# Second up-projection: seven products for eight in two of three token groups, and a plain group at the end

## The chip, the cores and the metric

One NeuronCore of a Trainium2 chip runs the whole program. The metric is device time in microseconds (us), the median of several runs. The engines are TensorE (PE, with its weight loads as PEld), VectorE (DVE), ScalarE (ACT), GpSimd (POOL, which only builds masks here) and SyncE (SP, whose queue issues all DMAs).

## What is computed

Chunked attention with eight memory keys, then two feed-forward layers on 3072 tokens of width 512, with an inner width of 2048, all in float32:

```python
out[:, :, c_start:c_end] = np.matmul(a, v_full)      # attention, per chunk of 32
...
h = x @ w_in;  r = np.maximum(h, 0.0);  g = s * (r * r) + b;  x = g @ w_out
...
h = x @ w_in2;  g = h - np.tanh(h);  return g @ w_out2
```

The change concerns `h = x @ w_in2` and `g = h - tanh(h)`, called **up 2** below. Before it stand attention, up 1 and **down 1** (`g @ w_out`), after it **down 2** (`g @ w_out2`).

## The kernel before

**Products.** A float32 operand is split in two float32r halves, a high one (ACT copies with rounding) and a low one (DVE subtracts the high one from the source). `three` (L149 to L152) multiplies with three matmuls of 128x512: high times high, low weight times high, high weight times low. A step on "one product" below means calls of `three`.

**Down 1 and down 2** (class `Down`, L447) use a two-by-two scheme of seven products P1 to P7 over halves of the inner and output dimensions. A pass p goes through one product for the three token groups g (1024 tokens each) in 12 entries of 12 matmuls. `run` (L608) issues for entry i: the split of entry i+2 (`split`, L554, ACT then DVE, into a ring of three buffers), a load of a later part (`load_to`, L495, SP), the matmuls (`multiply`, L571), then weight steps and `between`. The right-hand sides of down 2 were stored to `o2` by up 2 as seven combined operands and are loaded back as parts (p, g, h), where h is the half of the eight blocks n.

**Up 2** goes over eight blocks n of 256 columns of `w_in2` (L1016). In each block, groups g=0 and g=1 are computed plainly: per group two row tiles i and two columns `col`, each a `plain_column` (L934) of 4x3 = 12 matmuls, 48 in all; `plain_end` (L941) takes tanh on ACT and subtracts on DVE in tiles of 128x1024. Group g=2 is computed by `quad` (L959) as seven products of 6 matmuls, 42 in all. P1, P6, P5 and P3 accumulate in one PSUM bank, P7 and P4 in a second, P2 in a third, and snapshots of the first bank are copied out by ACT (L968) between them; DVE adds make the other outputs (L971), and each 128x512 output has its own tanh and subtract (L977, L978). The operands of P4 to P7 are sums of token quarters, T1 to T4, made on DVE at the end of down 1 (`b_t1` to `b_t3`, L666 to L674, and L698) and split by `t_split` (L861); the weight sums are made per block by `w2_sums` (L811) and split by `w2_split` (L823).

**Output of up 2.** `end_out` (L928) combines four outputs on DVE with four subtractions (`combine`, L437) and stores the pair of tiles `oa` and `ob`; two pairs are used in turn (`C_OT`). The eight PSUM banks are `bank(0)` to `bank(7)`; `bank2(2)` is banks 4 and 5, `bank2(3)` banks 6 and 7.

**What sets the order.** The program order of the kernel is the order on each engine (`manual_schedule`, L740); an instruction that waits holds all behind it on its engine. Tables place side work: `READY` (L64) prepares `w_out2` during down 1, `WEIGHTS` (L51) the weights of each pass.

```python
for n in range(8):
    ...
    for col in range(2):
        plain_column(n, 0, 0, col)
    ...
    group = quad(n)
```

Of the kernel before, what the change touches and what calls it, by code (L numbers as in the profile page):

```python
# [58 lines left out]
for q in (2, 5, 6):  # L59
# [24 lines left out]
def tile_chunk_attention_two_ffn(  # L84
# [86 lines left out]
    def filled_in_raw(z, raw):  # L171
# [21 lines left out]
    X2 = {"Q": ("E13", "E14", "E15"), "V": ("E16", "E17"),  # L193
          "X": (("Z9", "Z10"), ("Z2", "Z3"), ("Z4", "Z6")), "U": ("E6", "E7", ("Z0", "Z1"))}
    B_TMP = ("E16", "E17", "Z8")
    C_RAW, C_Z, C_W = "E0", "Z5", ("E1", "E2")
    C_OT = (("E3", "E11"), ("E9", "E12"))
    C_R = ("Y0", "Y1")
    C_T = {"T3": "E8", "T2": "E5", "T1": "E10", "T4": "E4"}
    C_SHL, C_SNAP = ("Y3", "Y4"), ("Y2", "Z7")  # L200
    Z2 = {("A11", 0): "Z8", ("A11", 1): "Y5", ("A21", 0): "Z11", ("A21", 1): "Z9",
          ("A22", 0): "Z10", ("A22", 1): "Z2", ("A12", 0): "Y3", ("A12", 1): "Y4"}
    D_WHL = (("E13", "E16"), ("E2", "E3"))
    D_STREAM = ("E6", "E17", "E14", "E7", "E11")
    D_RING = ("E8", "E5", "E10")
    D_S = (("Z4", "Z6"), ("Z0", "Z1"))
    D_ACC = {"X": ("Z7", "Z5", "Z3"), "U": ("Y0", "Y1", "Y2"), "V": ("E4", "E4", "E12")}
    D_OUT = ("E9", "E15")
# [238 lines left out]
    class Down:  # L447


        def __init__(self, src, zmap, smap, whl, stream, ring, load, view, pick, bias, final, turn):  # L450
# [4 lines left out]
            self.loaded, self.turn, self.ahead = 0, turn, 1 - 2 * turn  # L455
            self.parts = [(p, g, h) for p in range(7) for g in range(NG) for h in range(2)]
            self.entries = [(p, g, h, e) for p, g, h in self.parts for e in range(2)]
            self.quads = list(zmap)

        def load_quadrant(self, raw_place):  # L460
# [3 lines left out]
            def place_z():  # L464
                place = self.zmap[key]
                if isinstance(place, tuple):
                    if place[1] == 0:
                        self.zt[place[0]] = new(place[0], 2048, F32, "zq")
                    z = self.zt[place[0]][:, 1024 * place[1]:1024 * (place[1] + 1)]
                else:  # L470
                    z = new(place, 1024, F32, "zq")
                self.z[key] = z
                return z

            def begin():
                scaled(place_z(), raw)
# [12 lines left out]

        def load_words(self):  # L490
            key = self.quads.pop(0)
            z = self.z[key] = new(self.zmap[key], 1024, F32, "zq")
            nc.sync.dma_start(out=z, in_=wz[2 * ("A11", "A21", "A12", "A22").index(key[0]) + key[1]])

        def load_to(self, n):  # L495
            while self.loaded <= min(n, len(self.parts) - 1):
                i = self.loaded
                p, g, h = self.parts[i]
                self.part[i] = new(self.stream[i % len(self.stream)], 4 * NB, F32, "part")
                self.load(self.part[i], ORDER[p], g, h)  # L500
                self.loaded += 1
# [164 lines left out]
    def b_t3():  # L666
        b_f["T3"] = new(C_R[1], 2 * NB, F32, "t3").rearrange("p (m t) -> p m t", m=2)
        minus(b_f["T3"], b_f["Q"], b_f["V"])

    def b_t1():  # L670
        minus(b_f["V"], b_f["V"], b_f["X"])

    def b_t2():
        minus(b_f["Q"], b_f["Q"], b_f["V"])  # L674

    def final1(name, g, ps):
        a = lambda k: sums1.at(k, g)

        def last_sum(k, x, op):
# [5 lines left out]
            if g == NG - 1:  # L685
                b_f[k] = o
# [3 lines left out]
            def halves():  # L690
# [6 lines left out]
                if g == NG - 1 and k == "U":  # L697
                    minus(o, o, b_f["Q"])  # L698
# [27 lines left out]
        b_c[:, 0:1], final1, 0,  # L726
# [96 lines left out]
    def w2_split(n):  # L823
        hi, lo = (new(p_, 1024, F32R, "shl") for p_ in C_SHL)
# [23 lines left out]
    def between1(p, k):  # L848
# [37 lines left out]
    def final2(name, g, ps):  # L886
# [29 lines left out]
        None, final2, 1,  # L916
# [17 lines left out]
    def plain_column(n, g, i, col):  # L934
        ps = bank2(2 + i)
        wh, wl = wi[2, n]
        for c in range(KD):
            xh, xl = x2_of(c, 1 - col, g)
            three(ps[:, col, 0:NB], wh[:, i, c, :], wl[:, i, c, :], xh, xl, c == 0, c == KD - 1)

    def plain_end(n, g, i):  # L941
        ps = bank2(2 + i)
        oa = outs[n, g][0]
        r = new(C_R[i], 2 * NB, F32, "r2").rearrange("p (m t) -> p m t", m=2)
        nc.scalar.activation(out=r, in_=ps[:, :, 0:NB], func=AF.Tanh)
        nc.vector.tensor_tensor(out=oa[:, 2 * i:2 * i + 2], in0=ps[:, :, 0:NB], in1=r, op=ALU.subtract)
# [4 lines left out]
    def strassen(name):  # L951
        acc = bank(chain[name])
        wh, wl = w2_hl[name]
        xh, xl = x2[operand[name], NG - 1]
        new_ = name in ("P1", "P7", "P2")
        for c in range(2):
            three(acc, wh[:, c], wl[:, c], xh[:, c], xl[:, c], c == 0 and new_, c == 1, not new_)

    def quad(n):  # L959
        g = NG - 1  # L960
        begin_out(n, g)
        oa = outs[n, g][0]
        keep = new(C_SNAP[0], 2 * NB, F32, "keep")
        snap = {1: keep[:, 0:NB], 2: keep[:, NB:2 * NB], 3: new(C_SNAP[1], NB, F32, "keep3")}
        rs = {}

        def copy(q):
            nc.scalar.activation(out=snap[q], in_=bank(0), func=AF.Copy)  # L968

        def add(o, q, k):  # L970
            nc.vector.tensor_tensor(out=oa[:, o], in0=snap[q], in1=bank(k), op=ALU.add)  # L971

        def curve(o, src):
            if o // 2 not in rs:
                rs[o // 2] = new(C_R[o // 2], 2 * NB, F32, "r2").rearrange("p (m t) -> p m t", m=2)
            r = rs[o // 2][:, o % 2]
            nc.scalar.activation(out=r, in_=src, func=AF.Tanh)  # L977
            nc.vector.tensor_tensor(out=oa[:, o], in0=src, in1=r, op=ALU.subtract)  # L978

        strassen("P1")  # L980
        copy(1)
        yield
        strassen("P7")
        strassen("P6")
        copy(2)
        yield
        strassen("P5")
        copy(3)
        strassen("P2")
        add(2, 3, 1)  # L990
        strassen("P3")
        add(1, 1, 2)
        strassen("P4")
        yield
        curve(0, bank(0))
        curve(1, oa[:, 1])
        curve(2, oa[:, 2])
        add(3, 2, 1)
        curve(3, oa[:, 3])
        yield  # L1000
        end_out(n, g)
        yield

    group = None
# [11 lines left out]
    for n in range(8):  # L1016
        last = n == 7
        before = group
        begin_out(n, 0)
        for col in range(2):  # L1020
            plain_column(n, 0, 0, col)
        if before is not None:
            next(before)
        if not last:
            w2_load(n + 1)
        plain_end(n, 0, 0)
        if before is not None:
# [12 lines left out]
        begin_out(n, 1)  # L1040
# [25 lines left out]
        if last:  # L1066
            down2.split(0)
# [88 lines left out]
```

## Time and profile before

| | us |
|---|---|
| median of 3 runs | 1064.58 (1063.6 to 1066.26) |
| profiled execution | 1064.68 |
| its span, first to last instruction | 1062.7 |
| PE busy in the span | 1046.7 (98%) |
| DVE / ACT busy | 776.6 (73%) / 512.2 (48%) |
| granted clock of TensorE, mean | 0.997 |

The profiled execution is 0.10 us above the median. Busy time of PE counts matmuls that overlap, so a busy PE alone does not say that it is full; the distance from the start of one matmul to the next does. Up 2 runs from 579.6 to 829.9 us of the span, down 2 from there to the end.

### The profile page before, as it was taken

How to read it: one execution, taken by the hardware profiler on the slowest of the kernel's cores; microseconds unless marked ns; L12 is line 12 of the kernel's file. 1: busy time of each engine (PE TensorE's matmuls, PEld its weight loads, DVE VectorE, ACT ScalarE, POOL GpSimd, SP SyncE). 2: the span in 40 equal slices, each digit the busy share in tenths (PEclk: the TensorE clock that was granted, in tenths of full speed). 3: DMA queues.
4: the chain of work that ended last, by engine and by line, in shares of the span. 5: the costliest groups of instructions: out<-in, count | busy, mean ns of one | idle time of the engine just before them, and what ended most of it. 6: DMA issues, size and time to landing. Idle time of an engine off the chain costs nothing.

```text
span 1062.7 us, 15185 instructions
## 1 busy us (share of the span) xinstructions
PE 1046.7 (98%) x6048; PEld 867.8 (82%) x6048; DVE 776.6 (73%) x939; ACT 512.2 (48%) x914; POOL 2.8 (0%) x24
## 2 busy tenths in 40 slices
PE   6999999999999999999999999999999999999998
PEld 5788888888888888888888888888888888888887
DVE  7998557777657787878787767776766876776654
ACT  7886345444523564456554533333333554444432
POOL 1000000000000000000000000000000000000000
PEclk8999999999999999999999999999999999999999
DMA  9796378666458997666871266555557895556671
GB/s 320 246 336 244 137 271 293 242 246 214 178 210 316 358 338 277 206 227 221 288 261 41 98 239 247 218 208 198 213 202 272 322 374 190 192 185 248 228 267 60
DMA packets 74278, 250.54 MB, mean 236 GB/s; under 512 B 5600, under 2 KB 5856, under 8 KB 63968
## 3 DMA queue, kind: packets, MB, share of 16 engines
q1 hardware_dynamic: 74208, 249.58, 65.8%
q8 instruction: 47, 0.77, 0.3%
q14 instruction: 23, 0.19, 0.0%
HBM read 151.00 MB, written 98.57 MB: 235 GB/s over the span
## 4 chain that ended last, share of the span: by engine, by line
PE 95%; DMA 3%; DVE 1%; issue 0%; ACT 0%; SPq 0%; ACTq 0%
PE pb L150 30%; PE pb L152 30%; PE pb L151 30%; PE pb L323 2%; DMA raw<-in_wi_dram 2%; PE pb L301 2%; PE pb L261 1%; DMA part<-o 1%; DMA qk<-in_qk_dram 1%; DVE ringhringl L568 0%; ACT ringhringl L567 0%; DVE ob L439 0%; DVE oa L978 0%; DVE oa L971 0%; SPq L244 0%
## 5 line engine op out<-in xcount | busy, mean ns | idle before, releaser
L152 PE MATMUL pb<-ringhringl,whl 128*128 128x512 f32 (+1 forms) x680 | 262.9, 387 | 0.4 <-DVE ringhringl L568 0.4
L150 PE MATMUL pb<-ringhringl,whl 128*128 128x512 f32 (+1 forms) x680 | 262.9, 387 | 0.0
L151 PE MATMUL pb<-ringhringl,whl 128*128 128x512 f32 (+1 forms) x680 | 262.9, 387 | 0.0
L568 DVE TENSOR_TENSOR ringhringl<-part,ringhringl 128x1024 fp32r<-128x1024 f32 x120 | 146.7, 1224 | 81.9 <-ACT ringhringl L567 81.9
L567 ACT ACTIVATE ringhringl<-part 128x1024 fp32r<-128x1024 f32 x120 | 127.1, 1061 | 158.4 <-PE pb L152 151.3
L150 PE MATMUL pb<-xh,w 128*128 128x512 f32 (+1 forms) x392 | 153.9, 393 | 0.0
L152 PE MATMUL pb<-xl,w 128*128 128x512 f32 (+1 forms) x392 | 151.2, 386 | 0.0
L151 PE MATMUL pb<-xh,w 128*128 128x512 f32 (+1 forms) x392 | 151.0, 385 | 0.0
L152 PEld LDWEIGHTS pb<-ringhringl,whl 128*128 128x128 f32 x680 | 127.7, 188 | 26.6 <-DVE ringhringl L568 0.8
L150 PEld LDWEIGHTS pb<-ringhringl,whl 128*128 128x128 f32 x680 | 127.7, 188 | 26.0
L151 PEld LDWEIGHTS pb<-ringhringl,whl 128*128 128x128 f32 x680 | 127.7, 188 | 25.9
L414 ACT ACTIVATE r<-pb 128x512 f32<-128x512 f32 x96 | 55.4, 592 | 106.3 <-PE pb L152 93.5
L424 DVE SCALAR_TENSOR_TENSOR oa<-pb,s_c,r 128x512 f32<-128x512 f32 x96 | 70.6, 746 | 39.9 <-ACT r L414 39.7
L150 PEld LDWEIGHTS pb<-xh,w 128*128 128x128 f32 x392 | 73.6, 188 | 16.1
L285 ACT ACTIVATE sm<-sm,nmx 128x96 f32<-128x96 f32 x192 | 69.1, 362 | 36.4 <-DVE nmx L279 36.4
L152 PEld LDWEIGHTS pb<-xl,w 128*128 128x128 f32 x392 | 73.6, 188 | 15.0
L151 PEld LDWEIGHTS pb<-xh,w 128*128 128x128 f32 x392 | 73.7, 188 | 14.0
L150 PE MATMUL pb<-x2hx2l,w 128*128 128x512 f32 x192 | 74.7, 389 | 0.0
L151 PE MATMUL pb<-x2hx2l,w 128*128 128x512 f32 x192 | 74.7, 389 | 0.0
L152 PE MATMUL pb<-x2hx2l,w 128*128 128x512 f32 x192 | 74.7, 389 | 0.0
L562 ACT ACTIVATE ringhringl<-part,b_c 128x1024 fp32r<-128x1024 f32 x48 | 55.1, 1150 | 39.8 <-PE pb L152 37.3
L563 DVE SCALAR_TENSOR_TENSOR ringhringl<-part,b_c,ringhringl 128x1024 fp32r<-128x1024 f32 x48 | 61.5, 1283 | 16.9 <-ACT ringhringl L562 16.7
(134 smaller groups left out, 1351.4 us busy)
## 6 DMA issues: line engine op xcount, KB each, us to landing
o<-ob SPq DMA_DIRECT2D x48, 1024.0 KB, 4.8
part<-o SPq DMA_DIRECT2D x84, 512.0 KB, 4.9
part<-o SPq DMA_DIRECT2D x42, 1024.0 KB, 6.2
o<-oa SPq DMA_DIRECT2D x48, 768.0 KB, 3.4
raw<-in_wi_dram SPq DMA_DIRECT2D x16, 1024.0 KB, 7.8
raw<-in_wo_dram SPq DMA_DIRECT2D x16, 1024.0 KB, 7.9
qk<-in_qk_dram SPq DMA_DIRECT2D x24, 640.0 KB, 8.1
v<-in_vw_dram SPq DMA_DIRECT2D x24, 384.0 KB, 7.5
```

The costliest lines, as they stand in the source:

```text
L150: nc.tensor.matmul(acc, lhsT=whi, rhs=xhi, start=first, stop=False, skip_group_check=more)
L151: nc.tensor.matmul(acc, lhsT=wlo, rhs=xhi, start=False, stop=False, skip_group_check=more)
L152: nc.tensor.matmul(acc, lhsT=whi, rhs=xlo, start=False, stop=last, skip_group_check=more)
L285: nc.scalar.activation(out=sm[:, h, :], in_=sm[:, h, :], func=AF.Exp, bias=nmx[:, h:h + 1], scale=1.0, accum_out=sums[:, h:h + 1],)
L301: nc.tensor.transpose(out=bank(2 + g)[0:KE, P * r:P * (r + 1)], in_=sm[:, 4 * g + r, :], identity=ident)
L323: nc.tensor.matmul(value_bank(u)[64 * g:64 * g + 64, c0:c0 + QE], lhsT=tv[0:KE, e, 2 * r + g, :], rhs=pt[0:KE, 4 * g + r, QE * e:QE * (e + ...
L414: nc.scalar.activation(out=r, in_=up_ps[j, t], func=AF.Relu)
L424: nc.vector.scalar_tensor_tensor(out=oab[j, q][0][:, 2 * i:2 * i + 2, k, :], in0=ps2, scalar=s_c[:, 0:1], in1=r2, op0=ALU.mult, op1=ALU.mult,)
L562: nc.scalar.activation(out=xh, in_=src, func=AF.Identity, bias=self.bias)
L563: nc.vector.scalar_tensor_tensor(out=xl, in0=src, scalar=self.bias, in1=xh.bitcast(F32), op0=ALU.add, op1=ALU.subtract)
L567: nc.scalar.activation(out=xh, in_=src, func=AF.Copy)
L568: nc.vector.tensor_tensor(out=xl, in0=src, in1=xh.bitcast(F32), op=ALU.subtract)
```

## The change

Group g=1 of up 2 is computed by seven products as g=2 was; g=0 stays plain. The generator `quad` becomes a class `Quad` whose products, copies, adds, tanhs and subtractions are placed one by one. The two quads of a block, a and b, use banks 0, 1, 2 and banks 3, 7, 6; the second and third of b's are shared with the plain row tile 1. Snapshots 1 and 2 of both quads share one buffer (`C_SNAP`), snapshot 3 lies in `oa`; tanh is written into `ob` (or in place) instead of a buffer of its own. The next block's first plain column stands inside the quads of the block before. T1 to T4 exist for g=1 and g=2, so three more splits and four more sums are made; most are moved into passes 5 and 6 of down 1 (`SUMS`, `SPLITS`), and `READY` moves up. In the last block the plain group comes last, and down 2's first pass takes the groups in the order 1, 2, 0; its words of weights and its first parts are loaded at other places.

```diff
-    (3, 6): [("load", 5, "E7")], (4, 0): [("scale", 5, "Z9")], 
-    (4, 6): [("fill", 5), ("load", 6, "E7")], (4, 9): [("scale", 6, "Z0")], 
-    (5, 2): [("fill", 6), ("load", 7, "E7")], (5, 6): [("scale", 7, "Z1")], 
-    (5, 10): [("fill", 7)],
+    (3, 0): [("load", 5, "E7")], (3, 4): [("scale", 5, "Z9")],
+    (3, 8): [("fill", 5), ("load", 6, "E7")], (4, 2): [("scale", 6, "Z0")],
+    (4, 5): [("fill", 6), ("load", 7, "E7")], (4, 8): [("scale", 7, "Z1")],
+    (4, 11): [("fill", 7)],
 }
+SUMS = {(4, 9): [("T3", 1)], (5, 0): [("T3", 2)], (5, 9): [("T1", 1)], (5, 10): [("T2", 1)],
+        (6, 1): [("T1", 2)], (6, 2): [("T2", 2)]}
+SPLITS = {(5, 6): [("T3", 1)], (6, 5): [("T1", 1)], (6, 9): [("T4", 1)], (6, 10): [("T3", 2)], (6, 11): [("T1", 2)]}
...
-            self.parts = [(p, g, h) for p in range(7) for g in range(NG) for h in range(2)]
+            self.parts = [(p, g, h) for p in range(7) for g in (range(NG) if p else first) for h in range(2)]
...
+    banks = ((0, 1, 2), (3, 7, 6))
...
+        def place(self, q):
+            return self.oa[:, 2] if q == 3 else snap[0][:, NB * (q - 1):NB * q]
+        def copy(self, q):
+            nc.scalar.activation(out=self.place(q), in_=self.banks[0], func=AF.Copy)
+        def add(self, o, q, k):
+            nc.vector.tensor_tensor(out=self.oa[:, o], in0=self.place(q), in1=self.banks[k], op=ALU.add)
...
-    for n in range(8):
...
+    for n in range(7):
+        if n == 0:
+            plain_column(n, 0, 0)
+        plain_column(n, 0, 1)
...
+            last.add(3, 2, 1)
+            w2_split(n)
+            for o in (0, 1, 2):
+                last.tanh(o)
+            for o in (0, 1, 2):
+                last.curve(o)
+            plain_end(n, 0)
+            last.tanh(3)
+            last.curve(3)
+            last.end()
+            w2_steps[0](n + 1)
+        for col in range(2):
+            plain_column(n, 1, col)
+        w2_filled(n + 1)
...
+        plain_end(n, 1)
+        a, b = (Quad(n, g, k) for k, g in enumerate((2, 1) if n == 0 else (1, 2)))
+        a.mult("P1")
+        a.copy(1)
+        end_out(n, 0)
+        a.begin()
+        w2_high(n + 1)
+        a.mult("P7")
+        a.mult("P6")
+        a.copy(2)
+        a.mult("P2")
+        a.add(1, 1, 2)
+        a.mult("P5")
+        a.copy(3)
+        a.add(2, 3, 1)
+        b.mult("P1")
+        b.copy(1)
+        a.mult("P3")
+        w2_low(n + 1)
...
+        b.mult("P7")
+        w2_sums(n + 1)
+        a.mult("P4")
+        a.add(3, 2, 1)
+        b.mult("P6")
+        b.copy(2)
+        a.tanh(3)
+        a.curve(3)
+        b.begin()
+        b.mult("P2")
+        b.add(1, 1, 2)
+        b.mult("P5")
+        b.copy(3)
+        if n < 6:
+            plain_column(n + 1, 0, 0)
+        a.end()
+        b.add(2, 3, 1)
...
+        b.mult("P3")
+        b.mult("P4")
+        last = b
...
+    plain_column(7, 0, 1)
+    down2.split(0)
+    b.end()
+    down2.load_part(4)
+    begin_out(7, 0)
+    plain_end(7, 0)
+    for col in range(2):
+        plain_column(7, 1, col)
+    down2.split(1)
```

The curves left out above are, per output o, a tanh on ACT and a subtraction on DVE (`tanh`, `curve`).

The first place is DVE in the second half of block 2, at the end of its last quad. Before (`oa_5444`, `ob_5445`: the quad; `oa_5399`, `ob_5400`: group 1):

```order
L971 TENSOR_TENSOR oa_5444<-keep3_5447,pb_69 128x512
L971 TENSOR_TENSOR oa_5444<-keep_5446,pb_69 128x512
L439 TENSOR_TENSOR ob_5400<-oa_5399 128x512
L439 TENSOR_TENSOR ob_5400<-oa_5399,ob_5400 128x512
L439 TENSOR_TENSOR ob_5400<-oa_5399 128x512
L439 TENSOR_TENSOR ob_5400<-ob_5400,oa_5399 128x512
L978 TENSOR_TENSOR oa_5444<-pb_69,r2_5551 128x512
L978 TENSOR_TENSOR oa_5444<-oa_5444,r2_5551 128x512
L978 TENSOR_TENSOR oa_5444<-oa_5444,r2_5556 128x512
L971 TENSOR_TENSOR oa_5444<-keep_5446,pb_69 128x512
```

With the change (`oa_5422`, `ob_5423`: quad a; `oa_5500`: quad b):

```order
L673 TENSOR_TENSOR oa_5422<-pb_69,oa_5422 128x512
L822 TENSOR_TENSOR z_5377<-z_5377 128x256
L673 TENSOR_TENSOR z_5377<-z_5377 128x256 x3
L991 TENSOR_TENSOR oa_5422<-keep_5169,pb_69 128x512
L673 TENSOR_TENSOR oa_5422<-oa_5422,ob_5423 128x512
L991 TENSOR_TENSOR oa_5500<-keep_5169,pb_69 128x512
L445 TENSOR_TENSOR ob_5423<-oa_5422 128x512
L445 TENSOR_TENSOR ob_5423<-oa_5422,ob_5423 128x512
L445 TENSOR_TENSOR ob_5423<-oa_5422 128x512
L445 TENSOR_TENSOR ob_5423<-ob_5423,oa_5422 128x512
L991 TENSOR_TENSOR oa_5500<-oa_5500,pb_69 128x512
L991 TENSOR_TENSOR oa_5500<-keep_5169,pb_69 128x512
```

Quad a's last add (reading `keep_5169`) now stands behind the weight sums, and the add that frees quad b's second bank behind the four subtractions of quad a.

The second place is SP around the start of down 2 (`zq<-wz`: words of weights; `part<-o_g`: a part of group g; `o_g<-oa`, `o_g<-ob`: the stores of up 2). Before:

```order
L931 DMA o_0_87<-oa 128x1536
L932 DMA o_0_87<-ob 128x2048
L493 DMA zq<-wz_82 128x1024
L879 DMA part<-o_0_87 128x4x512
L493 DMA zq<-wz_85 128x1024
L879 DMA part<-o_0_87 128x4x512
L879 DMA part<-o_1_88 128x4x512
L931 DMA o_1_88<-oa 128x1536
L932 DMA o_1_88<-ob 128x2048
L879 DMA part<-o_1_88 128x4x512
L879 DMA part<-o_2_89 128x4x512
L931 DMA o_2_89<-oa 128x1536
```

With the change:

```order
L945 DMA o_1_88<-oa 128x1536
L946 DMA o_1_88<-ob 128x2048
L499 DMA zq<-wz_85 128x1024
L499 DMA zq<-wz_86 128x1024
L892 DMA part<-o_1_88 128x4x512
L945 DMA o_2_89<-oa 128x1536
L946 DMA o_2_89<-ob 128x2048
L892 DMA part<-o_0_87 128x4x512
L892 DMA part<-o_2_89 128x4x512
L945 DMA o_0_87<-oa 128x1536
L946 DMA o_0_87<-ob 128x2048
L892 DMA part<-o_0_87 128x4x512
```

The second half of each group's first part is loaded behind that group's last store, and the last pair of stores is now that of group 0.

## Rows read from the trace of the kernel before

**Rows 1.** The page's chain of work that ended last, by engine.
```profile
PE 95%; DMA 3%; DVE 1%; issue 0%; ACT 0%; SPq 0%; ACTq 0%
```

**Rows 2.** Waits of PE from 302 to 1059.3 us: total, times, longest.
```profile
PE pb L152 <- DVE ringhringl L568: 0.4, 1, 0.4
```

**Rows 3.** Timeline early in down 2: start, duration, instruction, [idle before <- releaser].
```profile
836.15 0.63 ACT L977 ACTIVATE r<-oa 128x512 f32<-128x512 f32 x1 [5.28 <-DVE oa L971]
836.68 2.94 ACT L567 ACTIVATE ringhringl<-part 128x1024 fp32r<-128x1024 f32 x3
...
838.28 0.39 PE L151 MATMUL pb<-ringhringl,whl 128*128 128x512 f32 x1
...
839.04 0.50 PE L152 MATMUL pb<-ringhringl,whl 128*128 128x512 f32 x1 [0.37 <-DVE ringhringl L568]
...
839.38 0.40 PE L150 MATMUL pb<-ringhringl,whl 128*128 128x512 f32 x1
```

**Rows 4.** Timeline around a plain column's end in up 2.
```profile
715.40 0.39 PE L152 MATMUL pb<-x2hx2l,w 128*128 128x512 f32 x1
...
715.83 1.03 ACT L945 ACTIVATE r<-pb 128x1024 f32<-128x1024 f32 x1 [3.40 <-PE pb L152]
...
716.89 1.23 DVE L946 TENSOR_TENSOR oa<-pb,r 128x1024 f32<-128x1024 f32 x1 [0.49 <-ACT r L945]
...
718.12 0.39 PE L152 MATMUL pb<-x2hx2l,w 128*128 128x512 f32 x1
```

**Rows 5.** Windows: length, busy (count) of PE, PEld, DVE, ACT, POOL; clock, DMA, GB/s.
```profile
514.30:547.00 32.70, 32.70 (x146) 27.05 (x146) 26.21 (x23) 18.60 (x17) 0.00 (x0) 1.00 0.75 253
547.00:579.60 32.60, 32.60 (x145) 27.02 (x144) 26.76 (x26) 15.81 (x15) 0.00 (x0) 1.00 0.39 134
579.60:610.90 31.30, 31.30 (x139) 25.90 (x138) 24.17 (x28) 14.77 (x18) 0.00 (x0) 1.00 0.21 84
610.90:642.20 31.30, 31.30 (x140) 25.91 (x139) 22.50 (x32) 11.11 (x16) 0.00 (x0) 1.00 0.63 228
829.90:857.10 27.20, 26.83 (x118) 21.88 (x117) 23.61 (x28) 13.59 (x15) 0.00 (x0) 1.00 0.90 325
302.00:1059.30 757.30, 756.93 (x3365) 627.21 (x3360) 552.32 (x584) 339.05 (x358) 0.00 (x0) 1.00 0.65 232
```

**Rows 6.** Timeline of DVE, 783 to 819 us.
```profile
783.12 0.69 DVE L163 TENSOR_SCALAR z<-z 128x1024 int32<-128x1024 int32 x1
...
791.21 1.34 DVE L664 TENSOR_TENSOR z<-z 128x256 f32<-128x256 f32 x3
...
796.80 0.68 DVE L439 TENSOR_TENSOR ob<-oa 128x512 f32<-128x512 f32 x1
797.52 0.69 DVE L439 TENSOR_TENSOR ob<-oa,ob 128x512 f32<-128x512 f32 x1
798.13 0.68 DVE L439 TENSOR_TENSOR ob<-oa 128x512 f32<-128x512 f32 x1
...
817.31 2.35 DVE L549 TENSOR_TENSOR whl<-zq,whl 128x1024 fp32r<-128x1024 f32 x2
```

**Rows 7.** Timeline of ACT, 805 to 831 us.
```profile
805.21 1.05 ACT L826 ACTIVATE shl<-z 128x1024 fp32r<-128x1024 f32 x1
...
821.91 0.60 ACT L968 ACTIVATE keep<-pb 128x512 f32<-128x512 f32 x1 [2.12 <-PE pb L152]
...
829.72 1.14 ACT L977 ACTIVATE r<-oa 128x512 f32<-128x512 f32 x2
```

**Rows 8.** DMA issues in up 2: count, KB each, median us from issue to landing.
```profile
o<-ob SPq DMA_DIRECT2D x22, 1024.0 KB, 4.8
o<-oa SPq DMA_DIRECT2D x23, 768.0 KB, 3.3
...
part<-o SPq DMA_DIRECT2D x3, 1024.0 KB, 10.5
```

More of the change, by code (lines that the diff above doesn't have):

```diff
@@ L447, in tile_chunk_attention_two_ffn, with __init__ @@
     class Down:
-        def __init__(self, src, zmap, smap, whl, stream, ring, load, view, pick, bias, final, turn):
+        def __init__(self, src, zmap, smap, whl, stream, ring, load, view, pick, bias, final, turn, ahead, first):
             self.src, self.zmap, self.smap, self.whl, self.stream, self.ring = src, zmap, smap, whl, stream, ring
@@ L664, in minus, with b_t3, b_t1, b_t2 @@
         nc.vector.tensor_tensor(out=out, in0=x, in1=y, op=ALU.subtract)
[L666 to L674, printed above, removed]
+    def b_t3(g):
+        minus(b_f["Q", g], b_f["Q", g], b_f["V", g])
+    def b_t1(g):
+        minus(b_f["V", g], b_f["V", g], b_f["X", g])
+    def b_t2(g):
+        nc.vector.tensor_tensor(out=b_f["X", g], in0=b_f["Q", g], in1=b_f["X", g], op=ALU.add)
     def final1(name, g, ps):
@@ L823, in w2_split @@
     def w2_split(n):
-        hi, lo = (new(p_, 1024, F32R, "shl") for p_ in C_SHL)
+        hi, lo = pair(C_SHL if n < 7 else C_SHL7, 1024, ("shlh", "shll"))
         z = w2_z.pop(n)
@@ L948, in tile_chunk_attention_two_ffn @@
     operand = {"P1": "X", "P2": "U", "P3": "Q", "P4": "T4", "P5": "T1", "P6": "T2", "P7": "T3"}
     chain = {"P1": 0, "P6": 0, "P5": 0, "P3": 0, "P7": 1, "P4": 1, "P2": 2}
[L951 to L976, printed above, removed]
-            nc.scalar.activation(out=r, in_=src, func=AF.Tanh)
[L978 to L1002, printed above, removed]
@@ L1004, in tile_chunk_attention_two_ffn, with __init__, begin, mult @@
-    group = None
+    banks = ((0, 1, 2), (3, 7, 6))
+    snap = []
+    class Quad:
+        def __init__(self, n, g, k):
+            self.n, self.g, self.banks = n, g, [bank(i) for i in banks[k]]
+        def begin(self):
+            begin_out(self.n, self.g)
+            self.oa, self.ob = outs[self.n, self.g]
+        def mult(self, name, cs=(0, 1)):
+            acc = self.banks[chain[name]]
+            wh, wl = w2_hl[self.n][name]
+            xh, xl = x2[operand[name], self.g]
+            new_ = name in ("P1", "P7", "P2")
+            for c in cs:
+                three(acc, wh[:, c], wl[:, c], xh[:, c], xl[:, c], c == 0 and new_, c == 1, not new_)
+        def place(self, q):
[4 more added lines that the diff above has]
+            nc.vector.tensor_tensor(out=self.oa[:, o], in0=self.place(q), in1=self.banks[k], op=ALU.add)
+        def tanh(self, o):
+            src, r = (self.oa[:, o], self.ob[:, o]) if o else (self.banks[0], self.oa[:, 0])
+            nc.scalar.activation(out=r, in_=src, func=AF.Tanh)
+        def curve(self, o):
+            src, r = (self.oa[:, o], self.ob[:, o]) if o else (self.banks[0], self.oa[:, 0])
+            minus(self.oa[:, o], src, r)
+        def end(self):
+            end_out(self.n, self.g)
@@ L1078, in between2 @@
-    def between2(p, k):
-        if p == 0 and k in (0, 2):
-            next(group)
-        if (p, k) in ((0, 3), (0, 7), (0, 8)):
+    last = None
+    for n in range(7):
+        if n == 0:
+            plain_column(n, 0, 0)
+        plain_column(n, 0, 1)
+        begin_out(n, 0)
+        if n == 0:
+            t_split("T2", 1)
+            t_split("T2", 2)
+            w2_split(0)
+            plain_end(n, 0)
+            t_split("T4", 2)
+            snap.append(new(C_SNAP, 2 * NB, F32, "keep"))
+            w2_load(1)
+            w2_steps[0](1)
+        else:
+            last.add(3, 2, 1)
[4 more added lines that the diff above has]
+                last.curve(o)
+            plain_end(n, 0)
+            last.tanh(3)
+            last.curve(3)
+            last.end()
+            w2_steps[0](n + 1)
+        for col in range(2):
+            plain_column(n, 1, col)
+        w2_filled(n + 1)
+        if n < 6:
+            w2_load(n + 2)
+        plain_end(n, 1)
+        a, b = (Quad(n, g, k) for k, g in enumerate((2, 1) if n == 0 else (1, 2)))
+        a.mult("P1")
+        a.copy(1)
+        end_out(n, 0)
+        a.begin()
[12 more added lines that the diff above has]
+        w2_low(n + 1)
+        for o in (1, 2, 0):
+            a.tanh(o)
+        for o in (1, 2, 0):
+            a.curve(o)
+        b.mult("P7")
[11 more added lines that the diff above has]
+        b.copy(3)
+        if n < 6:
+            plain_column(n + 1, 0, 0)
+        a.end()
+        b.add(2, 3, 1)
+        if n == 6:
+            w2_split(7)
+            c = Quad(7, 1, 0)
+            c.mult("P1")
+            c.copy(1)
+        b.mult("P3")
+        b.mult("P4")
+        last = b
@@ new lines, in tile_chunk_attention_two_ffn @@
+    a, b = c, Quad(7, 2, 1)
+    down2.load_words()
+    down2.load_words()
+    down2.load_part(0)
+    last.add(3, 2, 1)
+    a.begin()
+    for o in (0, 1, 2):
+        last.tanh(o)
+    a.mult("P7")
+    a.mult("P6")
+    last.tanh(3)
+    a.copy(2)
+    for o in range(4):
+        last.curve(o)
+    a.mult("P2")
+    a.add(1, 1, 2)
+    a.mult("P5")
+    a.copy(3)
+    last.end()
+    a.add(2, 3, 1)
+    b.mult("P1")
+    b.copy(1)
+    a.mult("P3")
+    for o in (1, 2, 0):
+        a.tanh(o)
@@ new lines, in tile_chunk_attention_two_ffn @@
+    for o in (1, 2, 0):
+        a.curve(o)
+    down2.load_words()
+    down2.load_words()
+    down2.load_part(2)
+    b.mult("P7")
+    a.mult("P4")
+    a.add(3, 2, 1)
+    for half in range(2):
+        down2.sums(0, half)
+        down2.high(0, half)
+    b.mult("P6")
+    b.copy(2)
+    a.tanh(3)
+    a.curve(3)
+    b.begin()
+    b.mult("P2")
+    b.add(1, 1, 2)
+    b.mult("P5")
+    b.copy(3)
+    plain_column(7, 0, 0)
+    a.end()
+    b.add(2, 3, 1)
+    for half in range(2):
+        down2.low(0, half)
@@ new lines, in tile_chunk_attention_two_ffn @@
+    down2.load_words()
+    down2.load_words()
+    down2.load_part(1)
+    b.mult("P3")
+    for o in (1, 2, 0):
+        b.tanh(o)
+    for o in (1, 2, 0):
+        b.curve(o)
+    b.mult("P4")
+    b.add(3, 2, 1)
+    b.tanh(3)
+    b.curve(3)
+    plain_column(7, 0, 1)
[7 more added lines that the diff above has]
+    down2.split(1)
+    def between2(p, k):
+        if p == 0 and k == 0:
+            plain_end(7, 1)
+        if p == 0 and k == 2:
+            end_out(7, 0)
+        if p == 0 and k in (4, 6):
```

187 lines of the change are left out of this document (70 added, 117 removed).

## The prediction

> **What bounds the kernel now.** I read the chain of waits first, then PE's waits, then its pace, and only then the load of the other engines. The chain [rows 1] is PE for 95% of the span, so time is won where PE issues less or waits less. PE's waits between 302 us and its last matmul [rows 2] are one single wait; everything else that PE ever waited for lies in the attention before it. Its pace comes from two matmuls of a plain column that stand twelve apart [rows 4]: 715.40 and 718.12, which is 2.72 us for twelve, or 0.2267 us each. The window over the same 757 us [rows 5] has PE idle for 0.37 us in all (a matmul's record overlaps the next, so starts show a gap better). So up 2 and down 2 last as long as their count of matmuls, and the question about this change is not what it saves on PE but whether ACT, DVE and the DMAs still keep PE from waiting.
>
> **What it removes.** A plain group is 48 matmuls per block, a quad 42. Eight blocks lose 6 each: 48 x 0.2267 = **10.88 us**. All of it lies on the path that sets the end as long as PE has no new gap. A block becomes 132 matmuls, 29.92 us, instead of 138, 31.28 us.
>
> **What it adds.** Per block DVE loses two subtractions of 128x1024 (1.23 us each [rows 4]) and gains three adds and four subtractions of 128x512 (0.68 us each [rows 6]): 22.50 us busy [rows 5] become 22.50 - 2.46 + 4.76 = 24.8 us of 29.92. ACT loses two tanhs of 1.03 us and gains three copies and four tanhs of 0.60 us [rows 4, 7]: 11.1 becomes 13.3 us. Both stay below PE, so they cost nothing unless one instruction is late. I therefore walk one block in order, with these prices: a reader of a PSUM bank starts 0.20 us after the last matmul's slot ends (that matmul starts at 715.40, its slot ends at 715.63, ACT starts at 715.83 [rows 4]); the subtraction starts as the tanh ends; one behind the other, DVE takes 0.60 us per 128x512, 0.72 where it reads the one before, 1.13 per 128x1024 0.45 per 128x256, and 0.60 for the integer shift [rows 6].
>
> Let 0 be the start of a block's second plain column. The slots of PE then end at 2.72, 5.44 and 8.16 (plain), aP1 9.52, aP7 10.88, aP6 12.24, aP2 13.60, aP5 14.96, bP1 16.32, aP3 17.68, bP7 19.04, aP4 20.40, bP6 21.76, bP2 23.12, bP5 24.48, the next block's first column 27.20, bP3 28.56, bP4 29.92. Four things can stop PE.
>
> First, the snapshots: between the end of P1, P6 or P5 and the next product into the same bank stands always one other product, 1.36 us; start and copy take 0.20 + 0.60, so 0.56 us are spare if ACT is free, and it is (the tanh of the plain tile before aP1's copy ends at 9.39, the copy starts at 9.72).
>
> Second, DVE at the start of the block: last add 0.2, weight split 0.8, three curves 1.9 to 3.7, plain subtraction 4.0 (its column ended at 2.72, its tanh at 3.95), last curve 5.1, four combines to 8.2, shift and fill of the next weights to 10.0, plain subtraction to 11.1, four combines to 13.6. That is just before aP2 ends. The bank pair of row tile 1 is free at 11.2, and bP7 wants it at 17.68; the split weights are there at 2.0, aP7 wants them at 9.52.
>
> Third, the shared snapshot buffer. aP5's copy ends at 15.8, then come a's add, the low weights and, held by b's first copy on ACT, the tanhs; the curves run from 17.6 to 19.4, the weight sums to 21.2, a's last add to 21.8. Quad b's second copy may overwrite the same half only then; it is ready at 21.96 from bP6. It ends at 22.56, and bP5 starts at 23.12.
>
> Fourth, b's second bank: a's last curve 23.1 to 23.7 (its tanh stands behind b's second copy), b's first add to 24.3, four combines to 26.8, b's add to 27.5. bP4 starts at 28.56, so 1.06 us are spare. After it the block repeats; DVE has stood still twice in between, so lateness does not build up.
>
> **The seams.** Opening: DVE gets four more sums and three more splits, 7 x 1.13 = 7.9 us, ACT 3 x 1.05 us. DVE stood still for 6.5 us in pass 5, 5.8 in pass 6 and 7.1 in block 0 [rows 5], and the moved preparation of `w_out2` takes two fills and a shift out of pass 5, some 2.9 us. The tightest place is entry 9 of pass 6: the final sum and weight sums of entry 7 end about 3.1 us into entry 8, entry 10's split at 4.3, the two pieces of U at 6.6, entry 11's split 5.0 us into entry 9; its low half is read 5.9 us in. After the last product of down 1 the queue is final sum, T1's split, U's split, the sum for T4, two splits of T2, the weight split: done some 8.2 us into block 0, and the first quad product wants them at 12.24. I cost the opening at nothing.
>
> Last quads: block 7's weight split starts on DVE behind b's add at 27.4 and ends at 28.6, while the product that reads its low half starts at 28.56 and needs it one matmul later, at 28.79. That is a tie; I take 0, at most 0.3.
>
> Down 2: counted on from block 6, the last plain column ends at 57.12 and entry 0 starts there. DVE is busy without a break from 50 on: split 0 ends at 54.1, b's combines at 56.5, the plain subtraction at 57.6, split 1 at 58.9, split 2 at 60.0. Entry 1 reads split 1's low half at 60.3, so 1.4 us are spare. Of the loads, that of group 0's first part waits on SP until the plain group's last matmul, 57.12, since it lands in that group's operand; group 2's second part stands behind it. With the 10.5 us that such loads took to land at this seam [rows 8], it lands at about 68.6, and entry 6 at 73.4 needs it some 2.3 us earlier. Group 0's second part stands behind its store, issued near 67.5, and lands near 78.4 for entry 10 at 84.3. The stores find their tiles free: a pair is reused two pairs later, at least 8 us after its store was issued, against landings of 3.3 and 4.8 us [rows 8].
>
> What goes away there is the wait in down 2 [rows 3]. Three starts, 838.28 to 839.38, take 1.10 us where two slots take 0.45: **0.65 us**. It came from ACT holding three splits behind a tanh that had waited 5.28 us for quad 7's last add. In the new order no quad is open when down 2 starts, so that wait has no cause; bounds are 0.65 gained and nothing gained.
>
> **Sum.** 1064.68 - 10.88 - 0.65 = 1053.15 for the profiled execution, which stood 0.10 us above the median: **1053.1 us**. What I cannot see is how exact the walk is. The nearest row for a late hand-over is that one of 0.65 us; the opening, block 7 and the start of down 2 could each have one like it, 0 to 1.95 us together. I take 0, because each has cover by the walk.
>
> **Rivals.** (1) *The second bank of quad b comes late in every block.* It hangs on the longest DVE queue, and the new order puts seven short instructions in place of two long ones. For it: only 1.06 us are spare. Against it: DVE overlaps the ends of its instructions, 0.60 us from start to start of 0.68 us long ones [rows 6]. If it came 1.76 us later, PE would lose 0.7 us in seven blocks: 1058.0 us. [...] I give it 0.08.
>
> (2) *The opening runs late.* If none of the seven added DVE instructions were covered, 7.9 us come back: 1061.0 us. For it: the three windows there have DVE already 77% to 82% busy. Against it: 19.5 us of idle time in them. 0.06.
>
> (3) *Slower: the shared snapshot buffer.* Quad b's second copy on ACT waits for a's last add on DVE, which stands behind the low weights, three curves and the weight sums; behind the copy stand a's tanh, a's curve, and so the rest of DVE's queue. From an end of that add at 22.5 on, 0.7 us later than I have it, each further us stops PE in all seven blocks. At 2.1 us beyond that, 7 x 2.1 = 14.7 us, the kernel is at 1067.8 and slower by 0.3%. For it: 2.9 us of other DVE work and three curves ahead of the add. Against it: DVE waits at four places earlier in the block, so its queue is empty there. 0.05, of which 0.03 slower and 0.02 near the old time.
>
> (4) *A load of down 2 comes late.* One entry lost, 2.72 us: 1055.8 us. 0.03.
>
> That the change does less than it says can be excluded: the program's matmuls are 48 fewer.
>
> **How the numbers follow.** The forecast has 0.78. About 0.3%, 3.2 us, is what a measurement of this kernel can tell from no change. Forecast, rivals 1, 2 and 4 all end below 1061.4, so faster is 0.95, same 0.02, slower 0.03. For the range I take the runs' spread downwards, 1 us: 1052.2. Upwards it takes the three unseen hand-overs, rival 4 and the nearer half of rival 1: 1056.4.
>
> **What would show it.** Right: no wait of PE after 302 us of more than 0.3 us; blocks of up 2 of 29.92 us; DVE about 24.8 us busy in each; down 2's first matmul near 819.0 us of the span instead of 829.9; no wait on a split in its first entries. Wrong: a wait of PE on a copy or add of a quad that comes back every 29.9 us (rivals 1 and 3), waits before 590 us (rival 2), or a wait on a split behind a DMA just after 819 us (rival 4).

## The result and the profile after

| | before | with the change |
|---|---|---|
| median, us | 1064.42 (1063.6 to 1066.26, 4 runs) | 1055.19 (1053.9 to 1057.27, 4 runs) |
| ratio, 95% interval | 1 | 0.9913 (0.9892 to 0.9934) |
| profiled execution / its span | 1064.68 / 1062.7 | 1053.9 / 1052.0 |
| first matmul of down 1, us of the span | 351.15 | 350.70 |
| down 1 / up 2 / down 2 to the end, us | 228.48 / 250.27 / 232.84 | 229.23 / 239.92 / 232.13 |

The kernel is 9.2 us faster in the median. A second timing (below) gives a ratio of 0.9900 (0.9884 to 0.9916) and 10.0 us. The profiled execution with the change is the fastest of its four. The two profiled executions differ by 10.78 us, and the last row splits the difference of their spans: -0.45 before down 1, +0.75 in down 1, -10.35 in up 2, -0.71 in down 2. Each stage runs from its first matmul to the first of the next.

PE's waits after the attention, the answer to [rows 2]:

```profile
PE pb L157 <- DVE ringhringl L572: 0.5, 1, 0.5
PE pb L155 <- DVE oa L991: 0.3, 1, 0.3
```

The wait in down 2 [rows 3] is gone; a wait on a split in down 1 and one on an add of a quad are new. (The view gives PE's idle time. What a wait costs is read below from the starts of matmuls, which comes out longer: 0.73 us for 0.46 in down 1.) The windows (columns as in [rows 5]): pass 6 of down 1, blocks 1 and 5 of up 2, the first ten entries of down 2, and everything after the attention:

```profile
547.30:579.90 32.60, 32.60 (x145) 27.02 (x144) 30.21 (x29) 19.71 (x19) 0.00 (x0) 1.00 0.37 130
...
612.56:642.48 29.92, 29.92 (x133) 24.77 (x132) 24.39 (x36) 12.80 (x20) 0.00 (x0) 1.00 0.59 220
732.24:762.16 29.92, 29.92 (x133) 24.77 (x132) 24.38 (x36) 12.81 (x20) 0.00 (x0) 1.00 0.59 220
819.80:847.00 27.20, 27.20 (x121) 22.52 (x121) 21.64 (x21) 14.30 (x14) 0.00 (x0) 1.00 1.01 370
302.00:1048.80 746.80, 746.08 (x3312) 617.90 (x3310) 574.85 (x631) 355.74 (x401) 0.00 (x0) 1.00 0.65 235
```

A block lasts 29.92 us with PE busy all through. DVE is 24.4 us busy in it (24.8 had been worked out), ACT 12.8. In pass 6 DVE rises from 26.76 to 30.21 of 32.6 us and PE loses nothing. Down 2 opens with full DMA engines, a share of 1.01 at 370 GB/s, where [rows 5] had 0.90 and 325.

**An ordinary block holds.** Timeline at the end of block 5, whose second plain column started at 732.24:

```profile
756.92 0.60 ACT L988 ACTIVATE oa<-pb 128x512 f32<-128x512 f32 x1 [1.56 <-PE pb L157]
...
758.54 0.68 DVE L445 TENSOR_TENSOR ob<-ob,oa 128x512 f32<-128x512 f32 x1
...
759.14 0.68 DVE L991 TENSOR_TENSOR oa<-oa,pb 128x512 f32<-128x512 f32 x1
...
760.80 0.39 PE L155 MATMUL pb<-t4h,w 128*128 128x512 f32 x1
```

Quad b's add ends at 759.82, 27.6 us into the block, where the walk had 27.5; P4 starts 28.56 us into it, as worked out. The time to spare, the cover, is 0.98 us.

**Block 6 does not.** The same place one block later:

```profile
786.84 0.60 ACT L988 ACTIVATE oa<-pb 128x512 f32<-128x512 f32 x1 [1.55 <-PE pb L157]
...
788.46 0.68 DVE L445 TENSOR_TENSOR ob<-ob,oa 128x512 f32<-128x512 f32 x1
...
789.06 0.68 DVE L991 TENSOR_TENSOR oa<-oa,pb 128x512 f32<-128x512 f32 x1
789.14 0.39 PE L157 MATMUL pb<-x2hx2l,shlh 128*128 128x512 f32 x1
...
789.79 0.19 PEld L155 LDWEIGHTS pb<-t4h,w 128*128 128x128 f32 x1 [0.69 <-DVE oa L991]
789.79 0.50 PE L155 MATMUL pb<-t4h,w 128*128 128x512 f32 x1 [0.27 <-DVE oa L991]
```

DVE is as punctual as before, but P4 wants the bank at 789.37: in block 6 the product of 1.36 us that begins block 7 stands where the other blocks have a plain column of 2.72 us. P4 starts 0.43 us late, and the next matmul another 0.11.

**Down 1.** Entry 11 of pass 4:

```profile
508.70 1.12 ACT L162 ACTIVATE zw<-raw 128x1024 f32<-128x1024 f32 x1 [4.33 <-DMA raw<-in_wo_dram]
509.73 3.22 ACT L571 ACTIVATE ringhringl<-part,b_c 128x1024 fp32r<-128x1024 f32 x3
...
510.91 1.28 DVE L572 SCALAR_TENSOR_TENSOR ringhringl<-part,b_c,ringhringl 128x1024 fp32r<-128x1024 f32 x1 [0.35 <-ACT ringhringl L571]
...
511.40 0.39 PE L156 MATMUL pb<-ringhringl,whl 128*128 128x512 f32 x1
...
512.11 1.22 DVE L673 TENSOR_TENSOR q<-q,sumV 128x1024 f32<-128x1024 f32 x1
...
512.25 0.50 PE L157 MATMUL pb<-ringhringl,whl 128*128 128x512 f32 x1 [0.46 <-DVE ringhringl L572]
```

ACT stands 4.33 us at the scaling of the last words of `w_out2`, whose load has not landed; three splits queue behind it, and the low half of the first of them (510.91) reaches PE 0.73 us late, counted over two starts. DVE's new sum for T3 (512.11) stands behind that low half.

### The profile page after: what moved, and what is told of

Its sections match the earlier page's. It is cut to its first block, busy times and chain, and to the rows that moved or that the text cites. A ratio compares the mean times of both kernels' runs of the same rounds, so it can differ in the third digit from the quotient of the medians.

```text
span 1052.0 us, 15226 instructions
## 1 busy us (share of the span) xinstructions
PE 1035.1 (98%) x6000; PEld 858.2 (82%) x6000; DVE 799.4 (76%) x986; ACT 529.1 (50%) x957; POOL 2.7 (0%) x24
## 4 chain that ended last, share of the span: by engine, by line
PE 95%; DMA 3%; DVE 1%; issue 0%; SPq 0%; ACT 0%; ACTq 0%
PE pb L155 30%; PE pb L157 30%; PE pb L156 30%; PE pb L329 2%; PE pb L307 2%; DMA v<-in_vw_dram 2%; PE pb L267 1%; DMA raw<-in_wi_dram 1%; DMA raw<-in_wo_dram 1%; DVE ob L445 0%; SPq L250 0%; DVE ringhringl L572 0%; DVE oa L991 0%; DVE whl L558 0%; ACT ringhringl L571 0%
## 5 line engine op out<-in xcount | busy, mean ns | idle before, releaser
L445 DVE TENSOR_TENSOR ob<-oa 128x512 f32<-128x512 f32 x96 | 65.6, 683 | 0.0
L155 PE MATMUL pb<-x2hx2l,w 128*128 128x512 f32 x112 | 43.6, 389 | 0.0
L156 PE MATMUL pb<-x2hx2l,w 128*128 128x512 f32 x112 | 43.6, 389 | 0.0
```

The costliest lines, as they stand in the source:

```text
L155: nc.tensor.matmul(acc, lhsT=whi, rhs=xhi, start=first, stop=False, skip_group_check=more)
L156: nc.tensor.matmul(acc, lhsT=wlo, rhs=xhi, start=False, stop=False, skip_group_check=more)
L445: sub = lambda o, x, y: eng.tensor_tensor(out=o, in0=x, in1=y, op=ALU.subtract)
```

## The experiments

**Is it the load, or DVE's new sum?** Two moves in the tables, one each:

```diff
-    (4, 5): [("fill", 6), ("load", 7, "E7")], (4, 8): [("scale", 7, "Z1")],
+    (4, 5): [("fill", 6), ("load", 7, "E7")], (4, 9): [("scale", 7, "Z1")],
```

> Theory L (a load not yet landed): the changed kernel's only wait of PE in down 1, about 0.6 us near 511 us, comes from ACT, which stood 4.33 us at the scaling of the last words of w_out2 (placed at entry 8 of pass 4) for their load; the splits of the ring queued behind it. With the scaling one entry later (entry 9) ACT waits 1.6 us there, 2.7 us less, and PE not at all before up 2; the wait in up 2 near 789 us (0.3 us) stays. Rival S (the new sum for T3 at entry 9 fills DVE): the wait in down 1 stays at 0.5 to 0.7 us.

```diff
-SUMS = {(4, 9): [("T3", 1)], (5, 0): [("T3", 2)], (5, 9): [("T1", 1)], (5, 10): [("T2", 1)],
+SUMS = {(4, 10): [("T3", 1)], (5, 0): [("T3", 2)], (5, 9): [("T1", 1)], (5, 10): [("T2", 1)],
```

> The sum for T3 of group 1 goes from entry 9 to entry 10 of pass 4, and nothing else moves. Theory L (a load not yet landed holds ACT): PE still waits 0.4 to 0.7 us near 511 us. Rival S (the new sum fills DVE): that wait is gone. Both: the wait near 789 us stays.

And the changed kernel again, unedited:

> The changed kernel once more, with more rounds. By the trace its stages changed by -10.35 us (up 2), -0.7 us (down 2) and +0.75 us (down 1), -10.3 us in all, and what stands before down 1 differs from run to run by some us either way. Theory: the median comes 9.5 to 11 us below the kernel before. Rival (the shorter up 2 costs something before down 1 as well): 8 to 9 us below, as in the first timing, 9.2.

Down 1 took 228.48 us in all three. ACT at that scaling, in the timelines of `scale7_one_entry_later`, `t3_sum_one_entry_later` and `changed_again`:

```profile
508.71 1.16 ACT L162 ACTIVATE zw<-raw 128x1024 f32<-128x1024 f32 x1 [0.20 <-DMA raw<-in_wo_dram]
```
```profile
507.60 1.12 ACT L162 ACTIVATE zw<-raw 128x1024 f32<-128x1024 f32 x1 [3.04 <-DMA raw<-in_wo_dram]
```
```profile
506.82 1.12 ACT L162 ACTIVATE zw<-raw 128x1024 f32<-128x1024 f32 x1 [3.38 <-DMA raw<-in_wo_dram]
```

The second expectation failed: with the sum moved the wait is gone too. But the unedited kernel has no wait in down 1 either, nor have the four other edited kernels below that leave this place alone: it came in one of six profiled executions of that order. So the missing wait in the first two runs tells nothing by itself. The traces of those six decide for the load. It is issued 149.94 us into down 1 in all of them; it took 7.99 us to land in the one with the wait and 6.50 to 7.15 us in the others, and ACT stood 4.33 us with it and 2.84 to 3.49 without. The new sum cannot have made that low half late: DVE had been idle for 0.35 us when it began, and did the sum behind it. Moving the scaling took ACT's stand to 0.20 us, less than the 1.6 expected, as the load also landed 1.35 us sooner in that run.

The second timing (1054.72 us, 1052.24 to 1055.02, 5 runs, against 1064.71 in 11) agrees with the theory: 10.0 us in the median, 10.6 by the ratio. What differs from run to run stands before down 1: its first matmul came between 349.8 and 354.0 us in the traces of this study.

**Block 6.** The add and block 7's weight split ahead of quad a's combines, in that block alone:

```diff
-        a.end()
+        if n < 6:
+            a.end()
         b.add(2, 3, 1)
         if n == 6:
             w2_split(7)
+            a.end()
```

> In block 6 alone the add that frees quad b's second bank, and the weight split of block 7, go ahead of quad a's four combines on DVE. Theory B (block 6 has the first product of block 7, 1.36 us, where the other blocks have a plain column, 2.72 us, so the walk's add, done at 27.5, meets P4 at 27.2 instead of 28.56): PE's wait on an add of a quad near 789 us is gone, some 0.5 us less from matmul start to matmul start; the wait near 511 us stays. Rival R (the bank is read late for another reason, such as the copy or ACT): the wait stays, or moves to block 7's first products.

The wait on the add is gone and up 2 takes 239.36 us, which is 1056 matmuls (1104 less 48) at 2.72 us for twelve. (The wait near 511 us did not stay, as said above.) Yet the span was no shorter: down 2 took 233.61 us, 1.48 more. The one wait that the view gives there, and the split on ACT that caused it:

```profile
PE pb L157 <- DVE ringhringl L577: 0.5, 1, 0.5
```
```profile
823.48 1.06 ACT L576 ACTIVATE ringhringl<-part 128x1024 fp32r<-128x1024 f32 x1 [6.41 <-DMA part<-o]
```

By the starts, PE is late three times in down 2, at 824.59, 825.85 and 837.09 us, by 0.30, 0.82 and 0.34 us: 1.46 in all. Quad a's store was issued 2.7 us later, at 791.90 instead of 789.17. The windows from 785 and 795 us, of the changed kernel and then of this one:

```profile
785.00:795.00 10.00, 9.73 (x43) 7.72 (x43) 8.61 (x13) 5.19 (x9) 0.00 (x0) 1.00 0.70 249
795.00:805.00 10.00, 10.00 (x46) 8.29 (x45) 6.44 (x11) 5.81 (x9) 0.00 (x0) 1.00 1.01 386
```
```profile
785.00:795.00 10.00, 10.00 (x46) 8.29 (x45) 8.83 (x14) 4.90 (x8) 0.00 (x0) 1.00 0.45 166
795.00:805.00 10.00, 10.00 (x46) 8.29 (x45) 6.96 (x12) 5.84 (x9) 0.00 (x0) 1.00 0.99 362
```

From 795 to 835 us the DMA engines are full in both, at shares of 0.99 to 1.03. Ten microseconds ahead of that they moved 249 GB/s or 166: what is not moved there is moved later. The eight transfers from the store issued at 798.81 (here 798.03) to the load at 809.67 (here 809.16) were issued 0.5 to 1.3 us earlier than in the changed kernel and landed 2.1 to 3.3 us later. The load that the late split reads is issued 0.06 us behind the landing of one of these stores in both traces, and so moves with it, from 811.79 to 815.07. So mending one wait made another. It is one run; the mechanism is read from its trace.

**Both mended.** The scaling at entry 9, and the add between the second and the third combine, so that the store goes only 0.6 us later:

```diff
...
+            combine(oa, ob, nc.vector, 0)
+            b.add(2, 3, 1)
+            combine(oa, ob, nc.vector, 1)
...
```

> The changed kernel with the last scaling one entry later (entry 9 of pass 4), and in block 6 the add that frees quad b's second bank between the second and the third of quad a's four combines. Theory: PE does not wait at all after the attention; down 1 228.5 us, up 2 239.36 us, down 2 232.1 us, 1.3 us less than the changed kernel in the trace, 0.5 to 2 us in the median; the store of quad a goes 0.6 us later instead of 2.7, so the loads of down 2 land in time. Rival D (any delay of that store shows, since the DMA engines are full from 795 to 835 us): a wait on a split of 0.2 us or more in the first entries of down 2.

```profile
302.00:1049.00 747.00, 747.00 (x3344) 619.04 (x3343) 575.94 (x631) 356.97 (x402) 0.00 (x0) 1.00 0.66 236
```
```profile
822.46 1.06 ACT L576 ACTIVATE ringhringl<-part 128x1024 fp32r<-128x1024 f32 x1 [4.25 <-DMA part<-o]
```

The view gives no wait of PE after the attention: 228.48, 239.49 and 232.13 us for the three stages, 1.2 us less than in the profile of the changed kernel (0.4 less than in `changed_again`, which had no wait in down 1). Up 2 is still 0.13 us above 239.36. Some 0.10 of it is block 7's weight split, whose low half, loaded as weights, makes the next matmul start 0.09 us late at 792.43. ACT does wait 4.25 us for the load, still inside its cover. The median is 1053.84 us (1050.76 to 1055.8, 6 runs), the ratio 0.9894 (0.9878 to 0.9910): the fastest kernel here, but its interval overlaps that of the changed kernel, so a gain over it shows in the stages alone, not in the medians.

**How much cover has quad b's second bank?** Its last combine three times more in blocks 0 to 5 (`extra` is 3 there):

```diff
...
+        for _ in range(extra):
+            minus(ob[:, 3], ob[:, 1], oa[:, 3])
...
```

> Quad a's last combine is done four times instead of once in blocks 0 to 5 (the same values again): 3 x 0.60 to 0.72 = 1.8 to 2.15 us more on DVE ahead of the add that frees quad b's second bank. Theory (the walk: that add has 1.0 us of cover in each of these blocks, and past it each us of DVE is a us of PE): PE waits 0.8 to 1.15 us in each of the six blocks on an add of a quad, matmul start to matmul start, 4.8 to 6.9 us in all. Rival (other cover or none): with more cover, no wait; with none, 1.8 us or more in each, 10.8 us.

Up 2 took 248.30 us, 8.4 more. PE's waits, and DVE in block 0:

```profile
PE pb L155 <- DVE oa L993: 6.8, 7, 1.1
```
```profile
610.32 2.15 DVE L673 TENSOR_TENSOR ob<-ob,oa 128x512 f32<-128x512 f32 x3
612.38 0.68 DVE L993 TENSOR_TENSOR oa<-oa,pb 128x512 f32<-128x512 f32 x1
```

The add starts 2.18 us later than the 610.20 it would have had. P4 starts 1.25 us late in each of the six blocks (1.36 with the next start), so 0.93 us were covered: the theory's 1.0, neither none nor more. The total is above the expected 4.8 to 6.9 us for three reasons: the repeats took 0.72 us each, the upper end of what was allowed for them; the cover was 0.07 us smaller; and the start behind each wait came 0.11 us later again. A subtraction of 128x512 lasts 0.68 to 0.69 us in this trace, but the queue goes by the distance of starts: 0.60 us from the third of the four combines to the fourth (609.00 to 609.60), which does not touch the output of the one before, and 0.72 from there to the first repeat (610.32), which writes it again.

**Does the shared snapshot buffer bind?** Quad a's last add three times, then the same with 512 elements of its own for quad b's second snapshot:

```diff
-        a.add(3, 2, 1)
+        for _ in range(3):
+            a.add(3, 2, 1)
```

> Quad a's last add is done three times in every block (the same values again), so it ends 1.2 to 1.45 us later. Theory (the snapshot buffer that both quads share makes quad b's second copy wait for it; the walk gives 0.7 us of cover before P5 of quad b stops): PE waits 0.5 to 0.75 us on a copy in each of blocks 0 to 6, 3.5 to 5 us in all. Rival (the copy does not hang on that add): no new wait on a copy.

```diff
...
+            if q == 2 and self.own:
+                return snap[1]
...
```

> As the run before, but quad b's second snapshot has 512 elements of its own. Theory (the shared buffer is the link): the waits on a copy are gone; what is left is lateness of DVE ahead of quad b's second bank, 1.2 to 1.45 us against 1.0 us of cover, so 0.2 to 0.5 us in each block on an add. Rival (the copy is late for another reason): the waits on a copy stay.

PE's waits of the first, then its block 0 (DVE and ACT, then PE); last, PE's waits of the second:

```profile
PE pb L155 <- ACT keep L988: 5.6, 7, 0.8
PE pb L155 <- DVE oa L991: 0.6, 1, 0.6
```
```profile
604.50 2.13 DVE L991 TENSOR_TENSOR oa<-keep,pb 128x512 f32<-128x512 f32 x3
606.74 0.60 ACT L988 ACTIVATE keep<-pb 128x512 f32<-128x512 f32 x1 [4.79 <-DVE oa L991]
```
```profile
606.19 0.39 PE L157 MATMUL pb<-x2hx2l,w 128*128 128x512 f32 x1
607.39 0.50 PE L155 MATMUL pb<-t1ht1l,shlh 128*128 128x512 f32 x1 [0.80 <-ACT keep L988]
```
```profile
PE pb L155 <- DVE oa L993: 1.1, 1, 1.1
```

ACT's copy starts 0.11 us after the third add ends; P5 starts 0.97 us late, in all seven blocks, and up 2 takes 8.1 us more. With the buffer apart, no copy holds PE, and up 2 takes 241.25 us, 1.3 more: 0.88 in block 6, whose add had no cover, and 0.06 to 0.08 in each of blocks 0 to 5. So the shared buffer is the link of rival 3, with 0.5 us of cover (1.45 us of lateness less 0.97) instead of the 0.7 worked out, which is why P5 was later than the 0.5 to 0.75 us expected. Of the 0.2 to 0.5 us expected on quad b's add in the second kernel, only those 0.06 to 0.08 came: the add ended up to 0.87 us later, 0.13 before P4's start, inside its cover but only just.

**What the wait of [rows 3] was.** Two edits of the kernel before. First the last add of the quad directly behind P4 (`add(3, 2, 1)` moved ahead of the `yield` and the curves):

> The kernel before, with the quad's last add on DVE right behind P4 instead of behind three curves. If its wait of 0.65 us in down 2 came from ACT holding three splits behind the tanh of that add, the tanh starts some 5 us earlier, the splits follow and the wait is gone: 0.6 us less. If it came from the parts' loads or from DVE's own load there, it stays at 0.4 us or more.

```profile
PE pb L152 <- DVE ringhringl L568: 0.5, 1, 0.5
```
```profile
832.57 1.77 ACT L977 ACTIVATE r<-oa 128x512 f32<-128x512 f32 x3
```
```profile
837.26 1.22 DVE L568 TENSOR_TENSOR ringhringl<-part,ringhringl 128x1024 fp32r<-128x1024 f32 x1
838.39 0.68 DVE L978 TENSOR_TENSOR oa<-pb,r 128x512 f32<-128x512 f32 x1
839.00 1.89 DVE L978 TENSOR_TENSOR oa<-oa,r 128x512 f32<-128x512 f32 x3
840.80 2.35 DVE L568 TENSOR_TENSOR ringhringl<-part,ringhringl 128x1024 fp32r<-128x1024 f32 x2
```

All tanhs are done by 834.4, no split of ACT queues behind one, and the wait is still there, 0.75 us by starts. DVE has entry 3's low split behind four subtractions of curves. But the edit also delayed DVE's queue: the add now stands there waiting 1.22 us for P4, and the four combines begin 1.94 us behind the first matmul of down 2 instead of 0.06. So the run shows that DVE's queue can make this wait without ACT; it does not show that it did so in the kernel before. There the same low split began with DVE idle, 0.03 us after ACT's high half ended:

```profile
837.76 2.36 DVE L568 TENSOR_TENSOR ringhringl<-part,ringhringl 128x1024 fp32r<-128x1024 f32 x2 [0.26 <-ACT ringhringl L567]
```

So in that trace ACT was the last link, as [rows 3] was read: its split stood behind a tanh, the tanh waited for the quad's last add, and the add stood on DVE behind three subtractions. The second edit puts all of the quad's curves, tanhs and last add included, one entry later:

```diff
-        if p == 0 and k in (0, 2):
+        if p == 0 and k in (1, 2):
```

> The kernel before, with quad 7's curves issued behind entry 1's matmuls of down 2 instead of entry 0's, so that on DVE the low split for entry 3 stands ahead of its four subtractions. If the wait of 0.65 us comes from DVE's queue (the split behind those subtractions), it is gone, 0.6 us less. If it comes from the parts' loads or from ACT, it stays at 0.4 us or more.

```profile
302.00:1057.00 755.00, 754.98 (x3350) 625.77 (x3350) 551.39 (x583) 338.56 (x357) 0.00 (x0) 1.00 0.65 232
```

The wait is gone, and the kernel took 1063.01 us. But down 2 took 232.44 us, 0.40 less and not the 0.6 expected: a later low split, behind DVE's four combines, now reaches PE 0.30 us late by the starts, with too little idle time for the view of waits:

```profile
841.59 2.35 DVE L568 TENSOR_TENSOR ringhringl<-part,ringhringl 128x1024 fp32r<-128x1024 f32 x2
...
842.86 0.50 PE L152 MATMUL pb<-ringhringl,whl 128*128 128x512 f32 x1
```

And since the tanhs moved together with the subtractions, the run does not tell ACT from DVE. What the two runs show is that the wait came from the quad's unfinished curves and last add standing ahead of entry 3's split, not from the parts' loads; how much of it was ACT's and how much DVE's stays open.

## Why the prediction was right, and where not

The forecast was 1053.1 us within 1052.2 to 1056.4; 1055.19 and 1054.72 lie in it, 2.1 and 1.6 us above the forecast.

- **48 matmuls x 0.2267 = 10.88 us**: right. Up 2 without its wait takes 239.36 us in `block6_add_first`, and blocks 0 to 5 of the changed kernel last 29.92 us each.
- **DVE and ACT in an ordinary block cost nothing**: right, and the walk held: 27.6 us for 27.5 at the end of the longest queue, 0.98 us of cover for 1.06, 24.4 us of DVE for 24.8; only the cover of the shared snapshot buffer was smaller, 0.5 for 0.7. The waits that rivals 1 and 3 name exist, and come as soon as lateness is added; without it they do not.
- **Four things can stop PE**: the fourth was checked against blocks 1 to 5 alone. The section on the seams counts block 6 on with P4 one product earlier, and there the add's 27.5 misses 27.20. The row of the walk was right and its deadline was read from the wrong block: 0.54 us lost (two starts). The tie at block 7's weight split, 0 to 0.3 us, gave nothing here, because P4's lateness put off the product that reads it; with P4 on time it gave 0.10 (`both_waits_mended`).
- **The opening costs nothing**: right for passes 5, 6 and block 0, of which it spoke; the moved preparation in pass 4 was named and not walked. It cost 0.73 us in the profiled execution and nothing in five others of the same order. So the prediction's own sign of rival 2, a wait before 590 us, showed (0.46 us of idle time at 512 us, where it allowed 0.3), but from a load landing late and not from the seven added DVE instructions.
- **0.65 us back in down 2**: right in size, -0.71. The cause given, ACT holding three splits behind a tanh, is the last link in the trace of the kernel before, but not all of it: without ACT's hold, and with DVE's queue put off by the same edit, the wait was as long. The new order has no open quad there, as the prediction said, and no wait.
- **The loads of down 2 land in time**: right, with less to spare than its separate landing times suggest, since the DMA engines are full there (a share of 0.99 to 1.03 from 795 to 835 us, in the changed kernel and in `block6_add_first`).

Summed, the trace lost 0.54 + 0.73 us against the forecast and gained 0.45 ahead of down 1, which is scatter, so that 1053.9 came close to 1053.15 in part by luck. That the median lies another 1.3 us above its profiled execution is within the runs' spread.

## What to carry to other kernels

When PE is dense, count the matmuls and then walk the other queues in order against PE's slots; it found the cover to 0.1 us at one place and to 0.2 at another here. Walk the irregular blocks too, first and last above all: a deadline moves when a neighbour in PE's order is shorter, as in block 6 (1.36 us for 2.72). And before an instruction on a store's path is delayed to mend a wait, look at whether the DMA engines are already full behind it, as they were here (a share of 0.99 to 1.03).

## What had not been expected of the hardware

At the seam of up 2 and down 2 the DMA engines ran at a share of 0.99 to 1.03 and 362 to 416 GB/s for 40 us (795 to 835 us, in the changed kernel and in `block6_add_first`), and a store issued 2.7 us later made later transfers land 2.1 to 3.3 us later in the second of them, although they were issued earlier. Behind each of PE's waits after the attention, in the kernel before (839.04 us) and in the changed kernel (512.25 and 789.79 us), the next matmul came 0.34 us after the one that had waited, 0.11 more than the 0.2267, so each of them cost that much more than the lateness of the matmul that waited.
